# Turning second and left blocks ahead of the next maxima, in a fused attention and MLP kernel

## The chip, the cores and the metric

The kernel runs on one core of one Trainium2 chip. The metric is the device time of one execution in microseconds (us). TensorE (PE) multiplies matrices, VectorE (DVE), ScalarE (ACT) and GpSimd (POOL) work element by element, and SyncE (SP) issues most of the DMA transfers. Each engine works through a queue of its own, and semaphores hold an instruction until its inputs are there.

## The reference

Two stages follow each other. The first is attention with a threshold, for 8 batches, 8 heads, 576 rows and a head size of 64, all in float32; the second is an MLP with a squared ReLU on the 4608 tokens that come out.

```
scores = scale * q @ k.T                                   # 576 x 576 for each head
thresh = max(scores, axis=-1) - tau
scores = where(scores >= thresh, scores, -1e9)
attn   = exp(scores - max(scores)); attn = attn / (sum(attn) + 1e-9)
x      = attn @ v                                          # -> 4608 x 512 tokens
out    = relu(x @ w_in) ** 2 @ w_out                       # w_in 512 x 2048, w_out 2048 x 512
```

## The kernel before, in words

The attention is done in **visits**. A visit takes two heads of a batch (`HP` = 4 such pairs of heads for each batch). The 576 rows are cut into four blocks of 128 (`NBLK` = 4) and a rest of 64. A **step** `s` handles one block of one visit: `steps[s]` is `(visit, block)`, and block number 4 stands for the rest. From visit 12 on (`paired`), two visits are taken together, and the rests of both visits make one block of 128 rows, the **left block**, which is the first step of the pair. A pair of visits so has nine steps: the left block, then blocks 0 to 3 of one visit and 0 to 3 of the other. These are the late steps, written by `late_step`; they begin at about 243 us of the profile. There are 12 such pairs, so 108 late steps, and some more after them that finish what is open. `NST` is the number of steps, and `END` is the step in which the last values are multiplied.

For each block and each of the two heads the work goes through the engines in this order:

- **Scores** (`scores_of_two`, L296, PE): the matmuls of q with k, into PSUM. An even block brings the scores of itself and of the odd block behind it; the odd step has none of its own.
- **Maxima** (`maxima`, L317, DVE): two reductions over 576 scores.
- **Exponents** (`exponents`, L340 to L343, ACT): two small operations on the maxima, and the exponential of both heads, with the maxima as bias.
- **Threshold** (`threshold`, L355 to L360, DVE): compares the scores with the threshold, multiplies the exponents with that, and sums.
- **Division** (`divide`, L365 and L367, POOL).
- **Turn** (`turn_blocks`, L459 to L469, DVE): transposes the divided block in squares of 32 x 32 into `turned`. A full block takes three or four transposes, a left block three.
- **Set-aside** (`set_aside`, L436): when the second block of two is turned, POOL issues a DMA that writes both from `turned` to DRAM, 1152 KB. `turn_last(s)` calls the turn for the block of step `s - 1` and, after an odd block, the set-aside.
- **Placing** (`place_blocks`): DMAs from SP read the two blocks back, in the order that the matmul needs, into `wT` (L477); a left block goes there straight from `turned` (L486).
- **Values** (`mix`, L530, PE): weights times v. ACT copies the result to `xT`, the tokens of the MLP (L513 to L524).

Between these, PE works on the MLP in **pieces** of some 1.8 us (`piece`, `fill`): sums of products with `w_in` (`unit`, L693) and with `w_out` (`product`, L799). What follows a piece on other engines is issued one piece later (`after`): ACT copies and squares (L701 to L729), additions on DVE (L705, L816 to L837), and sums of factors on POOL and DVE (L624), of which some stand in two waiting lists and are taken out one at a time (`some_later("gpsimd")`, `some_later("vector")`).

The order of each engine's instructions is the order in which the Python code issues them; no scheduler changes it. In a late step before the change, the code asks for the scores, the work behind the last piece, the maxima, one waiting operation of POOL, the exponents, then the turn of the last step's block if that was an odd block or a left block (`first`), pieces, threshold and division. If the last step's block was even, its turn comes later, behind this step's threshold. Only two buffers hold the weights of the blocks in turn (`w_slots`), so the exponents of step `s` need the turn of step `s - 2`.

Of the kernel before, what the change touches and what calls it, by code (L numbers as in the profile page):

```python
# [19 lines left out]
def kernel(  # L20
# [17 lines left out]
    NBLK = S // P  # L38
# [245 lines left out]
    def area(u, odd):  # L284
        at = AT[u, odd][0]
        return big[:, at:at + S].rearrange("p (h k) -> p h k", h=2)

    def scores_of_two(s):


        vis, i = steps[s]

        def term(u, odd, second_part, lhsT, keys, to=slice(0, P)):
            at, cut = AT[u, odd]
            x0, x1 = (cut, S) if second_part else (0, cut)
            nc.tensor.matmul(big[to, at + x0:at + x1], lhsT, keys[u * D:(u + 1) * D, x0:x1], start=True, stop=True)  # L296

        if i == NBLK:
            for x in range(2):
                for v_ in range(2):  # L300
                    for u in range(2):
                        cols = slice(v_ * D, (v_ + 1) * D)
                        term(u, 0, x != u, qmid[u * D:(u + 1) * D, cols], kT[v_], cols)
            return
        for at_, (u, odd, x) in enumerate(((1, 1, 0), (0, 0, 0), (1, 0, 1), (0, 0, 1), (1, 0, 0), (0, 1, 0), (1, 1, 1), (0, 1, 1))):
            at = (i + odd) * P
            term(u, odd, x, qT[u * D:(u + 1) * D, at:at + P], kT[vis % 2])
            if at_ == 0:
                nc.scalar.copy(seen, big[:, AT[1, 1][0]:AT[1, 1][0] + 1])

    def maxima(s, sc):
        vis, i = steps[s]
        n = len(sc)
        st = stats[s % len(stats)]
        mx = st[:, 0, 0:n]
        for u in range(n):
            nc.vector.tensor_reduce(out=mx[:, u:u + 1], in_=sc[u], axis=AX.XY, op=ALU.max)  # L317
        w = w_slots[(s - first_dma) % (2 if by_dma(vis) else 3)][:, 0:n, :]
        weights[vis, i] = w, sc, st
# [17 lines left out]
    def exponents(vis, i):  # L337
        w, sc, st = weights[vis, i]
        mx, thr, bias = (st[:, j, 0:len(sc)] for j in range(3))
        nc.scalar.activation(out=bias, in_=mx, func=AF.Copy, scale=-SCALE)  # L340
        nc.scalar.activation(out=thr, in_=mx, func=AF.Identity, bias=ntau8)
        for u in range(len(sc)):
            nc.scalar.activation(out=w[:, u, :].rearrange("p (h k) -> p h k", h=2), in_=sc[u],  # L343
                                 func=AF.Exp, bias=bias[:, u:u + 1], scale=SCALE)
# [88 lines left out]
    def set_aside(vis, pair):  # L433

        t = aside[len(outside) % 4]
        nc.gpsimd.dma_start(out=t, in_=turned[:, 0:NB])  # L436
        outside[vis, pair] = t.rearrange("(b r) (j x) -> r j b x", r=32, j=4)

    def turn_blocks(vis, i):

        w = weights[vis, i][0]
        two = i < NBLK
        M = KB - 2
        if not two or i % 2 == 0:
            lo = NB if paired(vis) else NB + NB // 2
            blocks[vis, i // 2] = (turned[:, 0:NB].rearrange("p (j c u q) -> p c j u q", j=4, u=2, q=32) if two  # L450
                                   else turned[:, lo:lo + NB // 2].rearrange("p (k q) -> p k q", q=32))
        wb = blocks[vis, i // 2]
        move = nc.vector.transpose
        if two:
            wb = wb[:, :, :, i % 2, :]
            whole_, rest_ = (w[:, :, x0 * 32:x1 * 32].rearrange("p u (c j q) -> p u c j q", q=32, j=n)
                             for x0, x1, n in ((0, M, 4), (M, KB, 2)))
            h = M // 4
            move(wb[:, 0:h, :, :], whole_[:, 0, :, :, :])  # L459
            if i < 2:  # L460
                move(wb[:, h, :, :].rearrange("p (u j) q -> p u j q", u=2), rest_[:, :, 0, :, :])
            else:
                move(wb[:, h, 2:4, :], rest_[:, 0, 0, :, :])
                move(wb[:, h, 0:2, :], rest_[:, 1, 0, :, :])
            move(wb[:, h + 1:, :, :], whole_[:, 1, :, :, :])  # L465
            return
        parts = [(0, 0, KB, 0), (1, M, KB, KB), (1, 0, M, KB + 2)] if paired(vis) else [(0, 0, KB, 2), (0, M, KB, 0)]
        for u, k0, k1, at in parts:
            move(wb[:, at:at + k1 - k0, :], w[:, u, k0 * 32:k1 * 32].rearrange("p (k q) -> p k q", q=32))  # L469
# [183 lines left out]
    def some_later(engine):  # L653
        if later[engine]:
            make(*later[engine].popleft())
# [201 lines left out]
    steps = [(n, i) for n in range(len(visits)) for i in visits[n][1]]  # L857
    NST = len(steps)

    def by_dma(n):  # L860

        return n >= 3 * HP - 1
# [7 lines left out]
    for s, (n, i) in enumerate(steps):  # L870
# [5 lines left out]
        if i in mixed:  # L876
            first, lag = mixed[i]
# [38 lines left out]
    def add_chunk(j):  # L916
        waiting.extend(pieces_of(j))
        whole.add(j)
# [27 lines left out]
    def after():  # L946
        now = state["last"]
        state["last"] = []
        for fn in state["then"]:
            state["last"] += fn() or []  # L950
        state["then"] = []
        for fn in now:
            fn()

    def piece():
        _, fn, *what = waiting.popleft()
        state["left"] -= PIECE_US
        state["made"] += 1
        if fn is mlp_out or what[0] <= PLAIN and what[1] == 0:
            after()  # L960
        then = fn(*what)
        after()
        state["then"] = then
        if state["step"] >= NST:
            some_later("vector")
            some_later("gpsimd")

    def fill(us):
        state["left"] += us
        while waiting and state["left"] >= PIECE_US / 2 and waiting[0][0] <= state["usable"]:  # L970
            piece()
        state["left"] = min(state["left"], PIECE_US)
# [77 lines left out]
    def turn_last(s):  # L1050
        if s <= NST:
            turn_blocks(*steps[s - 1])
            n, i = steps[s - 1]
            if i % 2 and by_dma(n) and goes_out(n, i // 2):
                set_aside(n, i // 2)

    def goes_out(n, pair):

        return pair < NBLK // 2
# [5 lines left out]
    def late_step(s):  # L1065

        on = s < NST
        odd = on and steps[s][1] % 2 == 1
        if on:
            n, i = steps[s]  # L1070
            if not odd:
                scores_of_two(s)
            after()
            maxima(s, [area(u, odd) for u in range(2)])
            some_later("gpsimd")
            exponents(n, i)
        first = s > NST or steps[s - 1][1] % 2 == 1 or steps[s - 1][1] == NBLK
        if first:
            turn_last(s)
        valued = s in mixes and s < END  # L1080

        todo = list(place_at[s])

        def place(all_):
            for what in list(todo):
                if all_ or not goes_out(*what[:2]):
                    place_blocks(*what)
                    todo.remove(what)

        if not valued:  # L1090
            place(False)

        def values():
            if s in mixes:
                while (visits[mixes[s][0]][0] // HP + 1) * S - RING > read_to["x"]:
                    piece()
                mix(*mixes[s])
                for j in chunk_at.get(s, ()):
                    add_chunk(j)

        if s == END:
            values()
        quarter = rate(s) / 4 if s < END else 1e9
        made = state["made"]
        fill(quarter)
        some_later("gpsimd")
        after()
        if on:
            threshold(n, i)
            divide(n, i)  # L1110
        if first:
            some_later("vector")
        fill(quarter)
        after()
        if not first:
            some_later("vector")
            turn_last(s)
        for fn in prep_at[s] + load_at[s]:
            fn()
        some_later("gpsimd")  # L1120
        if valued:
            at_least(1, made)
            made = state["made"]
            values()
        some_loads()
        place(True)
        some_later("vector")
        some_loads()
        fill(quarter)
        some_loads()  # L1130
        fill(quarter)
        some_loads()
        if valued:
            at_least(2, made)
            state["left"] = max(state["left"], -PIECE_US / 2)
# [55 lines left out]
    for s in range(END + 1):  # L1191
# [12 lines left out]
        on = s < NST  # L1204
# [130 lines left out]
```

## Time and profile before

| What | Value |
|---|---|
| Median of 3 runs | 1320.76 us (1320.71 to 1320.98) |
| The profiled execution | 1320.85 us, of which the span is 1319.1 us |
| TensorE | busy 1290.9 us, 98% of the span |
| VectorE | busy 936.9 us, 71% |
| GpSimd | busy 776.2 us, 59% |
| ScalarE | busy 585.4 us, 44% |
| POOL's wait at the set-aside for the turn (L436 for L465) | 177.5 us in 41 waits |
| DVE's wait at the maxima for the scores (L317 for L296) | 60.6 us in 47 waits |
| DVE's wait at the threshold for the exponents (L355 for L343) | 85.6 us in 58 waits |
| SP's wait at the placing for the set-aside (L477 for its landing) | 294.7 us in 42 waits |

A row of the timeline gives the start in us from the beginning of the span, the length, the engine, the line of the kernel, the operation with what it writes and reads, and in brackets how long the engine was idle before and what ended that. Matmuls overlap in the array, and their ends are modelled. Idle time of an engine costs nothing in itself; only what delays the last instruction does.

### The profile page before, as it was taken

How to read it: one execution, taken by the hardware profiler on the slowest of the kernel's cores; microseconds unless marked ns; L12 is line 12 of the kernel's file. 1: busy time of each engine (PE TensorE's matmuls, PEld its weight loads, DVE VectorE, ACT ScalarE, POOL GpSimd, SP SyncE). 2: the span in 40 equal slices, each digit the busy share in tenths (PEclk: the TensorE clock that was granted, in tenths of full speed). 3: DMA queues.
4: the chain of work that ended last, by engine and by line, in shares of the span. 5: the costliest groups of instructions: out<-in, count | busy, mean ns of one | idle time of the engine just before them, and what ended most of it. 6: DMA issues, size and time to landing. Idle time of an engine off the chain costs nothing.

```text
span 1319.1 us, 24730 instructions
## 1 busy us (share of the span) xinstructions
PE 1290.9 (98%) x8862; PEld 1070.6 (81%) x8862; DVE 936.9 (71%) x2034; ACT 585.4 (44%) x1353; POOL 776.2 (59%) x908
## 2 busy tenths in 40 slices
PE   7999999999999999999999999999999999999997
PEld 6676557897888888797978888888887988889997
DVE  6899776777777788788776877878686877522131
ACT  4887763244343526253435343525353434331331
POOL 3788874775747475556574746656574737455351
PEclk9999999999999999999999999999999999999999
DMA  6765431777777878686666768667676866520000
GB/s 127 156 181 145 126 73 60 145 173 168 165 173 178 181 177 186 143 200 160 170 157 158 158 154 187 172 137 185 146 173 139 198 162 161 144 53 9 9 17 17
DMA packets 320907, 185.48 MB, mean 141 GB/s; under 512 B 282224, under 2 KB 282256, under 8 KB 314384
## 3 DMA queue, kind: packets, MB, share of 16 engines
q1 hardware_dynamic: 309120, 115.78, 46.4%
q0 software_dynamic: 10000, 67.92, 12.9%
q8 instruction: 70, 1.15, 0.4%
q14 instruction: 53, 0.43, 0.1%
q10 hardware_dynamic: 1664, 0.21, 0.1%
HBM read 108.04 MB, written 68.42 MB: 134 GB/s over the span
## 4 chain that ended last, share of the span: by engine, by line
PE 83%; DVE 6%; DMA 3%; ACT 2%; issue 1%; POOL 1%; SPq 0%; DVEq 0%; POOLq 0%; ACTq 0%
PE big L693 29%; PE big L799 28%; PE big L530 10%; PE big L296 8%; PE big L579 3%; PE big L764 2%; PE big L280 2%; DVE st L317 1%; DMA wT<-aside 1%; DMA aside<-turned 1%; PE big L414 1%; DVE w L355 1%; ACT w L343 1%; DVE turned L154 0%; PE big L273 0%
## 5 line engine op out<-in xcount | busy, mean ns | idle before, releaser
L355 DVE SCALAR_TENSOR_TENSOR w<-big,st,w 128x576 f32<-128x576 f32 x269 | 207.4, 805 | 87.6 <-ACT w L343 85.6
L317 DVE TENSOR_REDUCE st<-big 128x1 f32<-128x576 f32 x288 | 204.1, 747 | 85.3 <-PE big L296 60.6
L367 POOL TENSOR_SCALAR w<-w,st 128x576 f32<-128x576 f32 x269 | 244.2, 916 | 29.4 <-DVE st L360 24.6
L799 PE MATMUL big<-wo,gsum 128*128 128x256 f32 x1088 | 243.8, 382 | 0.0
L799 PEld LDWEIGHTS big<-wo,gsum 128*128 128x128 f32 x1088 | 204.4, 190 | 37.0 <-issue 7.6
L693 PE MATMUL big<-xT,w_in_sb 128*128 128x128 f32 x1536 | 187.4, 277 | 1.5 <-DVE g L705 1.4
L693 PEld LDWEIGHTS big<-xT,w_in_sb 128*128 128x128 f32 x1536 | 178.5, 192 | 10.8 <-issue 7.7
L799 PE MATMUL big<-wo,g 128*128 128x256 f32 x816 | 185.3, 382 | 0.1
L343 ACT ACTIVATE w<-big,st 128x576 f32<-128x576 f32 x255 | 174.4, 735 | 0.2 <-issue 0.2
L799 PEld LDWEIGHTS big<-wo,g 128*128 128x128 f32 x816 | 151.6, 190 | 26.2 <-issue 6.5
L530 PE MATMUL big<-wT,vs 128*64 128x256 f32 (+5 forms) x1420 | 159.5, 389 | 4.9 <-DMA wT<-aside 3.5
L530 PEld LDWEIGHTS big<-wT,vs 128*64 128x64 f32 (+1 forms) x1420 | 86.0, 136 | 70.1 <-issue 20.8
L340 ACT ACTIVATE st<-st 128x2 f32<-128x2 f32 (+1 forms) x137 | 28.1, 205 | 253.3 <-DVE st L317 252.1
L365 POOL TENSOR_SCALAR st<-st 128x2 f32<-128x2 f32 (+1 forms) x148 | 35.6, 241 | 177.7 <-DVE w L355 167.1
L436 POOL DMA_DIRECT2D aside<-turned x50 | 29.9, 597 | 177.5 <-DVE turned L465 177.5
L705 DVE TENSOR_TENSOR g<-big,g 128x512 f32<-128x512 f32 x96 | 64.6, 676 | 83.7 <-PE big L693 78.1
L296 PE MATMUL big<-kT,qT 64*128 64x256 f32 (+3 forms) x768 | 107.0, 416 | 0.0
L296 PEld LDWEIGHTS big<-kT,qT 64*128 64x128 f32 x768 | 84.6, 186 | 14.5 <-issue 5.0
L701 ACT ACTIVATE g<-g 128x512 f32<-128x512 f32 x96 | 60.4, 630 | 63.5 <-DVE g L705 63.4
L569 POOL TENSOR_TENSOR gsum<-g 128x512 f32<-128x512 f32 x34 | 46.1, 1356 | 69.9 <-ACT g L702 69.6
L702 ACT ACTIVATE g<-g 128x512 f32<-128x512 f32 x128 | 80.9, 632 | 4.0
L459 DVE STREAM_TRANSPOSE turned<-w 128x512 f32<-128x512 f32 x100 | 70.2, 702 | 0.3 <-issue 0.3
(119 smaller groups left out, 2058.1 us busy)
## 6 DMA issues: line engine op xcount, KB each, us to landing
aside<-turned POOLq DMA_DIRECT2D x50, 1152.0 KB, 4.8
wT<-aside SPq DMA_DIRECT2D x200, 288.0 KB, 5.4
vs<-in_v_dram SPq DMA_DIRECT2D x72, 128.0 KB, 5.7
wo<-in_moe_w_in_dram SPq DMA_DIRECT2D x16, 512.0 KB, 4.8
wo<-in_moe_w_out_dram SPq DMA_DIRECT2D x16, 512.0 KB, 3.5
out_dram<-osb POOLq DMA_DIRECT2D x32, 256.0 KB, 3.9
kl<-in_k_dram SPq DMA_DIRECT2D x113, 72.0 KB, 2.8
ql<-in_q_dram SPq DMA_DIRECT2D x112, 72.0 KB, 5.7
```

The costliest lines, as they stand in the source:

```text
L296: nc.tensor.matmul(big[to, at + x0:at + x1], lhsT, keys[u * D:(u + 1) * D, x0:x1], start=True, stop=True)
L317: nc.vector.tensor_reduce(out=mx[:, u:u + 1], in_=sc[u], axis=AX.XY, op=ALU.max)
L343: nc.scalar.activation(out=w[:, u, :].rearrange("p (h k) -> p h k", h=2), in_=sc[u], func=AF.Exp, bias=bias[:, u:u + 1], scale=SCALE)
L355: nc.vector.scalar_tensor_tensor(out=wu, in0=sc[u], scalar=thr[:, u:u + 1], in1=wu, op0=ALU.is_ge, op1=ALU.mult, accum_out=sm[:, u:u + 1])
L367: nc.gpsimd.tensor_scalar(out=w[:, u, :], in0=w[:, u, :], scalar1=z[:, u:u + 1], scalar2=rcp[:, u:u + 1], op0=ALU.add, op1=ALU.mult)
L459: move(wb[:, 0:h, :, :], whole_[:, 0, :, :, :])
L530: nc.tensor.matmul(ps[u * D:(u + 1) * D, :], vs[n % 2][rows, u * (NBLK + 1) + c, :], wT[rows, at // REST:(at + ps.shape[1]) // REST, NBLK ...
L693: nc.tensor.matmul(to[:, f, :], factor(j, p, q, c)[:, f * P:(f + 1) * P], part[:, c, :], start=(p in "125" and f == 0 and c == 0), stop=(p ...
L701: nc.scalar.activation(out=to, in_=to if src is None else src, func=AF.Relu)
L702: nc.scalar.activation(out=to, in_=to, func=AF.Square)
L705: nc.vector.tensor_tensor(out=x, in0=to, in1=x, op=ALU.add)
L799: nc.tensor.matmul(to, left[:, f, :], wo[:, slot, f, :], start=(f == 0), stop=(f == HF - 1))
```

## The change

In `late_step`, the turn of a second block (an odd one) or of a left block is issued ahead of the maxima of the next step, and so also ahead of one waiting operation of POOL and of the exponents. The turn of an even block stays where it is. The very last block, whose turn was in the step behind the last one, is turned at the end of the last step, directly behind the turn of the block before it. PE, ACT and SP get the same instructions in the same order as before.

```diff
             if not odd:
                 scores_of_two(s)
             after()
+        first = s > NST or steps[s - 1][1] % 2 == 1 or steps[s - 1][1] == NBLK
+        if first and s != NST:
+            turn_last(s)
+        if on:
             maxima(s, [area(u, odd) for u in range(2)])
             some_later("gpsimd")
             exponents(n, i)
-        first = s > NST or steps[s - 1][1] % 2 == 1 or steps[s - 1][1] == NBLK
-        if first:
-            turn_last(s)
         valued = s in mixes and s < END
...
         if not first:
             some_later("vector")
             turn_last(s)
+            if s == NST - 1:
+                turn_last(NST)
         for fn in prep_at[s] + load_at[s]:
             fn()
```

## The prediction

> **What bounds the kernel now.** I read the page first, for the engine that is full; then the table of windows, for the stage in which it is full; then PE's own waits in that stage; then the timeline around some of the moved turns.
>
> ```profile
> PE 1290.9 (98%) x8862; PEld 1070.6 (81%) x8862; DVE 936.9 (71%) x2034; ACT 585.4 (44%) x1353; POOL 776.2 (59%) x908
> ```
>
> TensorE is full. In the window from 243 to 1158 us, the stage of paired visits that the change touches, it is busy for 910.71 of 915.00 us, so 4.29 us are idle there. From 1164.6 on only the MLP's matmuls are left, and PE runs them through. A stop of PE ahead of that point is therefore added to the time at the full, and a stop that is taken away is gained at the full. The question is which PE waits end sooner and which new ones arise.
>
> ```profile
> PE big L530 <- DMA wT<-aside: 2.8, 2, 1.6
> PE big L693 <- DVE g L705: 1.0, 1, 1.0
> PE big L693 <- POOL g L624: 0.7, 1, 0.7
> ```
>
> These are PE's waits from 500 us on (total us, times, longest). The first is what turning sooner could shorten; the timeline shows its two members at 549.96 (1.22 us) and 1162.07 (1.58 us), and one more of 0.69 us at 407.23.
>
> [...] at 825.27 ScalarE has stood idle 4.39 us for a maximum. So a late maximum holds up every copy behind it. [...] the page's DMA issues show a median of 4.8. The earlier start thus moves the landing, and does not shorten it.
>
> **The change part by part.** No instruction is added or removed. On PE, ACT and SP the order is the same; on DVE and POOL only places change.
>
> *Part 1, 60 turns go ahead of maxima.* They are one left block from the visit before the stage, 12 left blocks of the pairs, and 47 second blocks (48 less the very last). One turn lasts 1.49 us (L459 0.70, L461 0.27, L465 0.67, overlapping a little), 1.54 with four pieces.
>
> ```profile
> 823.53 0.38 DVE L837 TENSOR_TENSOR osb<-big,osb 128x256 f32<-128x256 f32 x1
> 823.84 1.40 DVE L317 TENSOR_REDUCE st<-big 128x1 f32<-128x576 f32 x2
> 825.17 0.68 DVE L459 STREAM_TRANSPOSE turned<-w 128x512 f32<-128x512 f32 x1
> 825.78 0.26 DVE L461 STREAM_TRANSPOSE turned<-w 128x128 f32<-128x128 f32 x1
> 825.98 0.66 DVE L465 STREAM_TRANSPOSE turned<-w 128x512 f32<-128x512 f32 x1
> 826.57 0.77 DVE L355 SCALAR_TENSOR_TENSOR w<-big,st,w 128x576 f32<-128x576 f32 x1
> ```
>
> ```profile
> 825.27 0.21 ACT L340 ACTIVATE st<-st 128x2 f32<-128x2 f32 x1 [4.39 <-DVE st L317]
> 825.57 1.37 ACT L343 ACTIVATE w<-big,st 128x576 f32<-128x576 f32 x2
> 826.82 0.59 ACT L713 COPY g<-big 128x512 f32<-128x512 f32 x1
> ```
>
> In this place (columns: start, length, engine, line) VectorE turns while ScalarE makes the exponents: the turn is hidden under 1.9 us of ScalarE work, and the threshold follows it at once. With the turn first, maxima, exponents and the copy L713 all come 1.5 us later, VectorE then waits for the exponents, and the threshold comes 1.3 us later. PE needs L713's copy at 827.56, 0.15 us after its end.
>
> What hides the moved turn in its new place is VectorE's wait for the scores. For each of the 60 I took from the timeline when VectorE was free, when the division (L367) was done, and when the maximum began; the new maximum begins a turn after the later of the first two. In 9 places the wait covers the turn; in 51 the maximum comes later; the mean over all is 0.93 us. The threshold, which today starts when the turn ends and about 0.3 us after the first exponent, comes 0.58 us later in the mean. VectorE is busy 698 of 915 us here, so most of this is caught up in its waits for PE. It costs where PE needs something queued behind: a copy of ScalarE behind the exponents (L713, L718, L725), a VectorE result behind the threshold (L705, L837, kT), or GpSimd work behind the division (L624).
>
> I set each such lateness against the time between the result's end and PE's start on it, in the trace of before. PE has 659 waits on these engines in the stage and after; on DVE 18, ACT 18 and POOL 7 results lie less than 1 us ahead of their use. Where the lateness is more than that, the rest is a stop of PE, at (us): 278.5 L837 0.49; 436.5 L718 0.87; 507.4 L718 0.93; 761.1 kT 1.10; 767.6 L725 1.05; 827.6 L713 1.44; 893.2 L624 1.05; 905.5 L713 0.60; 965.8 L713 1.55; 1042.2 L718 0.59; three small ones 0.27. Sum: 9.9 us lost.
>
> *The DMAs of part 1.* Each of the 47 second blocks has a 1152 KB set-aside (L436) that GpSimd issues; it also goes ahead of one queued GpSimd operation (some 1.3 us for an L624). The turn ends 2.0 us sooner in the mean, so GpSimd waits less at L436 (177.5 us in all today), but what stood between may now wait for the turn. SP's queue keeps its order, and most of its waits are for these landings (294.7 us in 42 waits at L477), so it comes free sooner. For the two transfers that PE waits for, the turn starts 2.13 us earlier (392.79 and 535.00 today), more than 0.69 and 1.22: both stops go. Gain 1.9 us.
>
> *Part 2, the last block.* Today its turn stands behind L816, which waits for PE:
>
> ```profile
> 1144.41 0.42 DVE L816 TENSOR_TENSOR osb<-big,held 128x256 f32<-128x256 f32 x1 [2.96 <-PE big L799]
> 1144.75 0.70 DVE L459 STREAM_TRANSPOSE turned<-w 128x512 f32<-128x512 f32 x1
> ```
>
> ```profile
> 1146.59 0.60 POOL L436 DMA_DIRECT2D aside<-turned  x1 [4.82 <-DVE turned L465]
> ```
>
> The division ends at 1141.77 and the turn before it at 1141.45, so it can start at 1141.8, 2.9 us sooner. GpSimd is idle, and SP has already waited at L477. PE's stop of 1.58 us at 1162.07 goes unless the transfer is slowed: this one took 7.7 us to land beside four L477 transfers and will overlap them longer. Bounds of the gain: 0 and 1.58; I take 1.58, as 1.3 us are to spare. Work behind the turn on VectorE is L816, which waits for PE until 1144.4 anyway: cost nothing.
>
> *Sum.* 9.9 - 1.9 - 1.6 = +6.4 us on the profiled execution's 1320.85 (span 1319.1, and 1.75 around), which is 0.09 above the median of 1320.76. That gives 1327.2; I say 1327.
>
> The lateness that I took for the turn is bounded below by nothing (VectorE's slack takes it, as in 9 places) and above by the full 1.54 us. The waits of the turn on GpSimd are not fully shown: in 18 of 60 places the division ends after VectorE is free, by 1.2 us at 900.86, and it may itself be late after a late threshold. Bounds of the lost sum: 2 us, if a stop of PE gives the next places room and VectorE catches up, and 15, if lateness also reaches the second maximum of a pair and the next scores (L296 starts within 1.6 us of the end of the threshold it waits for in 19 places).
>
> **Rivals.** *Hidden, and the transfers gain* (ends on the other side): VectorE waits for scores ahead of maxima in 49 of the 60 places, 60.6 us at L317 over the whole run, and the turn fits in; PE loses under 0.8 us and wins 3.5: 1317.3. Against it are the 11 places without any such wait, where there is no room, and the short reserves at 827.6 and 965.8. It decides if the losses stay under 0.8 us. Chance 0.09.
>
> *Halved*: the stops lie close together (761 and 768, 893 and 905, 1022 to 1042) and the first makes room for the second; about 4 to 5 us lost, 3.5 won: 1322. For it: the stop at 761.1 moves all that PE needs later by 1.1 us. Chance 0.16.
>
> *Runs on*: the division comes late too, GpSimd holds the turn, and VectorE stops with everything behind it: 15 lost, 3.5 won, 1332. For it: GpSimd works without a wait from 880 to 888. Chance 0.15.
>
> That the change does not do what it says is excluded: in the built program's order the turns stand ahead of the maxima.
>
> **How the numbers follow.** My forecast has 0.60. A measurement of this kernel can tell 0.2%, or 2.6 us, from no change, so faster is under 1318.1 and slower over 1323.4. Slower: forecast 0.60, the late rival 0.15, and a little of the halved one, 0.77 in all; same 0.14; faster 0.09. The range runs from 1319.5 (losses of 2 us beside the gains, the lower bound) to 1332.5 (losses of 15 with gains of 3.5).
>
> **What would show it.** Right: PE waits of 0.5 to 1.5 us at L693 behind ACT copies L713, L718 and L725; VectorE's wait at L355 for ACT rising from 85.6 us by some 35 (60 times about 0.6); L436's wait on the turn falling below 177.5; the wait for wT<-aside gone from PE. Wrong: PE idle in the stage still at 4 us, or the L530 stops still there.

## The result, and the profile after

| | Median | Runs |
|---|---|---|
| Before | 1320.74 us | 4 runs, 1319.98 to 1320.98 |
| After | 1329.99 us | 4 runs, 1329.04 to 1331.56 |

The change makes the kernel slower by 0.7%: the ratio of after to before is 1.0072, with a 95% interval of 1.0055 to 1.009. The profiled execution of after took 1330.07 us, of which the span is 1328.3 us, against 1320.85 and 1319.1 before. The forecast was 1327 us, slower.

The first line of the page of after gives each engine's busy time, its share of the span and its instructions:

```profile
PE 1296.2 (98%) x8862; PEld 1073.7 (81%) x8862; DVE 941.6 (71%) x2034; ACT 581.7 (44%) x1353; POOL 776.9 (58%) x908
```

TensorE has 5.3 us more of busy time for the same 8862 matmuls. Two windows of 3.41 us at half clock, at 59 and 428 us, make some 2.9 us of it (the delays of 1.27 and 1.62 us in the table below). I put the rest down to parts of stops: the modelled end of the matmul ahead of a stop covers a little of it (at 827.6 PE becomes 1.28 us late, but counts as idle for 0.99). In the stage itself, from 243 to 1166 us of after, PE is busy for 912.91 of 923.00 us, so 10.09 us are idle, where it was 4.29. Of PE's waits in after, over the whole run, those that the change bears on (us in total, times, longest):

```profile
PE big L693 <- DVE g L705: 2.4, 1, 2.4
...
PE big L693 <- ACT g L713: 2.1, 2, 1.1
PE big L693 <- POOL g L624: 2.0, 3, 0.9
...
PE big L693 <- ACT g L718: 1.3, 2, 0.8
```

The wait for `wT<-aside`, 3.5 us in three waits before, is gone altogether. In its place stand waits for copies of ScalarE and for GpSimd's sums, as forecast (one of 1.1 us for kT is in the same list), and one stop of 2.4 us behind VectorE's L705, which was not in the forecast. The waits of all engines in after show how the order of work shifted:

```profile
DVE w L355 <- ACT w L343: 140.3, 114, 3.8
...
POOL aside L436 <- DVE turned L465: 88.1, 32, 6.3
...
DVE st L317 <- PE big L296: 11.9, 11, 1.9
```

VectorE's wait for the scores (L317) fell from 60.6 to 11.9 us: the turns now stand in that wait. Its wait for the exponents (L355) rose from 85.6 to 140.3 us: the turns no longer stand in that one. The same work has moved from one hole to another, and what lies between the two holes (maxima, exponents, the copies behind them) is late. GpSimd waits 89 us less at the set-aside, and 88 us more at L365 for the threshold (255.3 us for 167.1).

The place that the prediction showed, in the timeline of after (start, length, engine, line; in brackets the wait and what ended it):

```profile
830.42 0.69 DVE L459 STREAM_TRANSPOSE turned<-w 128x512 f32<-128x512 f32 x1
...
831.82 1.38 DVE L317 TENSOR_REDUCE st<-big 128x1 f32<-128x576 f32 x2
...
833.53 1.36 ACT L343 ACTIVATE w<-big,st 128x576 f32<-128x576 f32 x2
...
834.29 0.82 DVE L355 SCALAR_TENSOR_TENSOR w<-big,st,w 128x576 f32<-128x576 f32 x1 [1.09 <-ACT w L343]
...
834.78 0.59 ACT L713 COPY g<-big 128x512 f32<-128x512 f32 x1
...
835.42 2.05 PE L693 MATMUL big<-t,g 128*128 128x128 f32 x16 [0.99 <-ACT g L713]
```

The turn stands ahead of the maxima. L343 begins 1.71 us behind their start, as before (1.73), but VectorE has nothing to do until then and waits 1.09 us. The copy L713 ends at 835.37, just ahead of PE's start: PE has stopped for 0.99 us. Part 2 of the change in the same view:

```profile
1152.39 0.67 DVE L459 STREAM_TRANSPOSE turned<-w 128x512 f32<-128x512 f32 x1
...
1154.21 0.60 POOL L436 DMA_DIRECT2D aside<-turned  x1 [1.41 <-DVE turned L465]
...
1155.44 0.42 DVE L816 TENSOR_TENSOR osb<-big,held 128x256 f32<-128x256 f32 x1 [1.53 <-PE big L799]
```

The last turn follows the one before it (its L465 ends at 1152.47) without a gap, and stands ahead of L816; the set-aside goes out 1.2 us ahead of L816, where it was 2.2 us behind it.

**Where the 9.25 us come from.** PE's instructions have the same order in both kernels, so the start of each can be set against the start of the same one before. The shift between the two grows or falls only in a few places. At the end it is 9.25 us. That the medians differ by the same figure (1329.99 - 1320.74) is chance, since the four runs of after spread over 2.5 us. Places are named by their time before, with the line whose wait changed there.

| Place (us) | Forecast | Measured |
|---|---|---|
| 278.5, L837 | +0.49 | +0.34 |
| 373.9, scores L296 | none | +0.68 |
| 407.2, transfer | -0.69 | -0.81 |
| 423.4, L705 | none | +1.94, and +1.62 behind it |
| 436.5, L718 | +0.87 | 0 |
| 507.4, L718 | +0.93 | +0.79 |
| 550.0, transfer | -1.22 | -1.43 |
| 761.1, kT | +1.10 | +1.28 |
| 767.6, L725 | +1.05 | +0.93 |
| 827.6, L713 | +1.44 | +1.28 |
| 893.2, L624 | +1.05 | +1.15 |
| 905.5, L713 | +0.60 | 0 |
| 965.8 L713, and 968.8 behind it | +1.55 | +1.37 - 0.94 |
| 1032.9, L624 | not named | +0.56 |
| three small ones, places not given | +0.27 | not told apart |
| 1042.2, L718 | +0.59 | +1.04 |
| 1162.0, transfer | -1.58 | -1.78 |
| 445.4 to 493.6, and 820.0 | none | -0.26 + 0.22 |
| 59.5 to 60.6, ahead of the change | none | +1.27 |
| Sum | +6.4 | +9.25 |

The last place lies in the first stage, which the change does not touch. It is a variation between runs: it is there in three of the fourteen traces of this study, two of them of experiments. So about 8 us of this pair of traces are the change's own; the interval of the ratio, 7.3 to 11.9 us, holds this.

The largest term is the one that the forecast lacked, at 423 us. The timelines show what happened there. Before:

```profile
419.23 1.28 POOL L624 TENSOR_TENSOR gsum<-w_in_sb,g 128x512 f32<-128x512 f32 x1
...
419.91 1.16 DVE L624 TENSOR_TENSOR gsum<-w_in_sb 128x512 f32<-128x512 f32 x1
...
423.43 2.05 PE L693 MATMUL big<-xT,w_in_sb 128*128 128x128 f32 x16 [0.44 <-DVE g L705]
```

After:

```profile
421.43 2.50 POOL L624 TENSOR_TENSOR gsum<-w_in_sb,g 128x512 f32<-128x512 f32 x2
...
421.90 2.58 DVE L624 TENSOR_TENSOR gsum<-w_in_sb 128x512 f32<-128x512 f32 x1
...
426.85 2.90 PE L693 MATMUL big<-xT,w_in_sb 128*128 128x128 f32 x16 [2.38 <-DVE g L705]
```

GpSimd makes two sums L624 in both; before, the first began at 417.43. VectorE's own L624 took 1.16 us before and takes 2.58 after; it ends 0.56 us after the end of GpSimd's second one in both (421.07 and 420.51; 424.48 and 423.93). Then come one more L624, L705, and PE, which has stood 2.38 us instead of 0.44. The 16 matmuls from 426.85 on take 2.90 us instead of 2.05. The table of windows tells why, with three stretches of after (start, end and length; busy us and instructions of PE, PEld, DVE, ACT and POOL; then the granted clock):

```profile
424.44:427.85 3.41, 1.04 (x10) 1.01 (x10) 3.41 (x6) 0.99 (x2) 3.24 (x5) 1.00 0.77 235
427.85:431.26 3.41, 3.41 (x19) 3.41 (x18) 1.68 (x4) 2.90 (x7) 2.18 (x2) 0.50 1.01 234
431.26:434.68 3.41, 3.41 (x30) 3.27 (x31) 3.07 (x10) 0.00 (x0) 1.85 (x3) 1.00 1.17 197
```

In the window that holds the stop, PE is busy for 1.04 of 3.41 us. In the next, just as long, it runs at a clock of 0.50 and has 19 matmuls, where the window after it has 30. That is the 1.62 us behind the stop, and it is the busy time that grew.

### The profile page after: what moved, and what is told of

Its sections match the earlier page's. It is cut to its first block, busy times and chain, and to the rows that moved or that the text cites. A ratio compares the mean times of both kernels' runs of the same rounds, so it can differ in the third digit from the quotient of the medians.

```text
span 1328.3 us, 24730 instructions
## 1 busy us (share of the span) xinstructions
PE 1296.2 (98%) x8862; PEld 1073.7 (81%) x8862; DVE 941.6 (71%) x2034; ACT 581.7 (44%) x1353; POOL 776.9 (58%) x908
## 3 DMA queue, kind: packets, MB, share of 16 engines
q8 instruction: 70, 1.15, 0.4%
## 4 chain that ended last, share of the span: by engine, by line
PE 79%; DVE 10%; ACT 3%; issue 2%; POOL 1%; DVEq 0%; ACTq 0%; POOLq 0%
PE big L799 27%; PE big L693 26%; PE big L530 10%; PE big L296 7%; PE big L579 3%; DVE st L317 3%; PE big L280 2%; DVE w L355 2%; PE big L764 2%; ACT w L343 2%; PE big L414 1%; DVE gsum L823 1%; DVE turned L465 1%; DVE turned L459 1%; POOL w L367 0%
## 5 line engine op out<-in xcount | busy, mean ns | idle before, releaser
L355 DVE SCALAR_TENSOR_TENSOR w<-big,st,w 128x576 f32<-128x576 f32 x269 | 209.6, 815 | 142.1 <-ACT w L343 140.3
L367 POOL TENSOR_SCALAR w<-w,st 128x576 f32<-128x576 f32 x269 | 244.6, 918 | 30.9 <-DVE st L360 27.0
L317 DVE TENSOR_REDUCE st<-big 128x1 f32<-128x576 f32 x288 | 202.6, 741 | 37.1 <-PE big L280 23.0
L693 PE MATMUL big<-xT,w_in_sb 128*128 128x128 f32 x1536 | 188.6, 278 | 3.8 <-DVE g L705 2.4
L365 POOL TENSOR_SCALAR st<-st 128x2 f32<-128x2 f32 (+1 forms) x148 | 35.6, 241 | 264.8 <-DVE w L355 255.3
L693 PEld LDWEIGHTS big<-xT,w_in_sb 128*128 128x128 f32 x1536 | 179.2, 192 | 13.3 <-issue 7.3
L343 ACT ACTIVATE w<-big,st 128x576 f32<-128x576 f32 x255 | 173.9, 732 | 0.2 <-issue 0.2
L705 DVE TENSOR_TENSOR g<-big,g 128x512 f32<-128x512 f32 x96 | 65.1, 680 | 80.4 <-PE big L693 74.1
L296 PE MATMUL big<-kT,qT 64*128 64x256 f32 (+3 forms) x768 | 107.5, 416 | 0.2 <-DVE w L355 0.2
L296 PEld LDWEIGHTS big<-kT,qT 64*128 64x128 f32 x768 | 84.7, 186 | 15.2 <-issue 3.6
L436 POOL DMA_DIRECT2D aside<-turned x50 | 29.8, 595 | 94.5 <-DVE turned L465 88.1
```

What stands on the lines that cost most here:

```text
L355: nc.vector.scalar_tensor_tensor(out=wu, in0=sc[u], scalar=thr[:, u:u + 1], in1=wu, op0=ALU.is_ge, op1=ALU.mult, accum_out=sm[:, u:u + 1])
L367: nc.gpsimd.tensor_scalar(out=w[:, u, :], in0=w[:, u, :], scalar1=z[:, u:u + 1], scalar2=rcp[:, u:u + 1], op0=ALU.add, op1=ALU.mult)
L693: nc.tensor.matmul(to[:, f, :], factor(j, p, q, c)[:, f * P:(f + 1) * P], part[:, c, :], start=(p in "125" and f == 0 and c == 0), stop=(p ...
L705: nc.vector.tensor_tensor(out=x, in0=to, in1=x, op=ALU.add)
```

## The experiments

The expectations call a turn a transpose, and a sum L624 a multiply-add. Two questions were open: whether the listed stops are really caused by the ten moves that the forecast put them down to, and what brought the stop at 423 us. In the experiments the moves of part 1 are counted from 0 to 59; `firsts` is the list of their steps. All ratios are to runs of the kernel before on the same chip, with 95% intervals.

### The ten moves, back and alone

The ten moves behind the ten listed stops were left in their old place, and all else of the change kept:

```diff
+    firsts = [s for s in range(first_late, NST) if steps[s - 1][1] % 2 == 1 or steps[s - 1][1] == NBLK]
...
-        if first and s != NST:
+        ahead = first and s < NST and firsts.index(s) not in (2, 13, 18, 34, 35, 39, 43, 44, 48, 53)
+        if ahead:
             turn_last(s)
...
             exponents(n, i)
+        if first and s != NST and not ahead:
+            turn_last(s)
```

> The change, but at the ten moves where the prediction placed a stop of TensorE (numbers 2, 13, 18, 34, 35, 39, 43, 44, 48 and 53 of the 60) the turn stands behind the maxima again; 50 moves and the last block's turn remain. Theory (lateness costs only where TensorE needs something queued behind, so the loss sits in these ten places): in the trace after, the stops there sum to about 8.2 us, and a stop of 0.9 at 968.8 comes back, so 7 us less than the change, about 1323. Rival (the lateness is spread over all moves, each costing its share of some 13 us): a sixth of that, 2 us less, about 1328.

Then those ten alone went ahead (`in` for `not in`), without part 2:

> Only these ten turns are ahead of the maxima; the other 50 and the last block stay as before. Theory of the ten places: about 7 us slower than before, 1328, without the two gains at the values (407 and 550) and at the end. Rival of spread lateness: 2 us slower, 1323.

Measured: with the ten taken back, 1319.98 us (12 runs), ratio 0.9999 (0.9991 to 1.0008). The ten alone: 1328.92 us (4 runs), ratio 1.0061 (1.0046 to 1.0076). Of PE's waits with the ten alone:

```profile
PE big L530 <- DMA wT<-aside: 3.0, 3, 1.2
```

Ten moves of sixty make a loss nearly as large as the whole, with the same waits for L713 as in after (2.1 us in two), and leave the transfers' stops. Shift by place: 436.5 +0.73, 507.4 +0.79, 761.1 +1.18, 767.6 +0.94, 827.6 +1.27, 893.2 +1.17, 965.8 +1.41 less 0.95 behind it, 1042.2 +0.43. Together that is 7.0 us at eight of the ten places. At 278.5 only 0.18 came, at 905.5 nothing, and 0.44 at 445.4, which no list had.

The other fifty and part 2 cancel out, but not because each costs nothing. In their trace the transfers' stops are gone (-0.90, -1.42 and -1.79 us at 407, 550 and 1162), while the stop at 423 is there at its full, 2.51 us (+2.04, and +1.4 of half clock behind it), and the scores at 373.9 and the sum at 1032.9 are late by 0.59 and 0.57. The kernel is 3 us faster than I had expected, and only one of these shows in the traces: the profiled run of 1322.01 us is 8.06 below after's 1330.07, where 7 were expected, and some 0.8 of that lie in the first stage. The median is 2.0 us lower still. Each run has its own granted clock on record: the three at 0.995 or 0.996, the profiled one among them, took 1322.0 to 1322.6 us, the nine at 0.997 or 0.998 took 1318.7 to 1320.4. So most runs seem to be without one of the half-clock windows; no trace of such a run is kept, so this is not shown.

### Part 1 alone, part 2 alone

```diff
         if not first:
             some_later("vector")
             turn_last(s)
-            if s == NST - 1:
-                turn_last(NST)
```

with the last turn at its old place in the step behind is part 1 alone; the turn of before with these two lines is part 2 alone.

> The 60 moves without the last block's earlier turn. Theory: TensorE's stop of about 1.6 us for the last wT transfer is back, so 1.6 to 2 us slower than the change: about 1331.8. Rival (the earlier turn only overlaps the transfer with others, and the last values wait all the same): as the change, 1330.

> The last block's turn directly behind the one before it, and no other move. Theory: the stop of 1.58 us at 1162 is gone and nothing else differs: 1319.0, 0.12% faster than before. Rival: the set-aside, overlapping the transfers before it, lands no sooner: 1320.7.

Part 1 alone took 1331.6 us (4 runs, 1327.04 to 1331.88), ratio 1.0071 (1.0047 to 1.0094); the stop at the last transfer is back, 1.38 us. Part 2 alone took 1319.05 us (20 runs), ratio 0.999 (0.9984 to 0.9997); in its trace only this stop is gone. So part 2 is worth 1.3 to 1.6 us, as forecast, and the loss is part 1's. In the profiled run of part 1 alone the stop at 423 is there with 2.44 us, but no half clock follows it; one follows two stops for GpSimd's L624 at 900 us instead (PE loses 2.8 us there, where the others with the ten moves lose some 1.2), as it does in the kernel of the next section with the set-aside at its old place.

### The stop at 423 us: two theories that fell

My first theory was that GpSimd's set-aside, moved ahead of one queued sum, had left its two sums L624 back to back, and VectorE's sum without a place between them. In the first test the turns go ahead as in the change, but the set-aside keeps its old place:

```diff
-        if first and s != NST:
-            turn_last(s)
+        if first and s < NST:
+            turn_blocks(*steps[s - 1])
...
             some_later("gpsimd")
             exponents(n, i)
+            if first and steps[s - 1][1] % 2:
+                set_aside(steps[s - 1][0], steps[s - 1][1] // 2)
```

> VectorE's transposes go ahead of the next maxima as in the change, but the set-aside on GpSimd keeps its old place in GpSimd's order, one multiply-add later. Theory (the stop of 2.4 us at 423 us comes of GpSimd running two multiply-adds back to back beside VectorE's, which takes 2.58 us in place of 1.16): that stop goes, with it 2.0 us and the half-clock window behind it of about 1.6 us, and the kernel takes about 1326.4 us. Rival (the stop comes of VectorE's own order, the transpose ahead of the maxima): it stays, and the kernel takes 1330 us like the change.

My second theory put the stop down to the move beside it, no. 12, at 415 us. It was taken back along with the ten, and tried alone:

```diff
+        ahead = first and s < NST and firsts.index(s) not in (2, 12, 13, 18, 34, 35, 39, 43, 44, 48, 53)
```

> As the kernel with ten moves taken back, with move no. 12 (at 415 us) taken back too. Theory (the stop at 423 us hangs on that one move): 1319.98 - 2.0 = 1318 us, and to 1316.5 us where the half-clock window behind that stop goes with it. Rival (it hangs on the moves ahead of it, which put VectorE and GpSimd at another time): it stays, 1320 us.

```diff
+        ahead = first and s < NST and firsts.index(s) == 12
```

> The kernel before with move no. 12 (at 415 us) alone. Theory (that one move brings the stop at 423 us): 1320.5 + 2.0 = 1322.5 us, and up to 1324 us with a half-clock window behind the stop. Rival (the prediction's tally, which gave that move no cost): 1320.5 us.

Measured: with the set-aside at its old place 1329.15 us (4 runs), ratio 1.006 (1.0046 to 1.0074); with no. 12 taken back too 1320.51 us (13 runs), ratio 1.0002 (0.9993 to 1.001); with no. 12 alone 1320.49 us (12 runs), ratio 1.0002 (0.9994 to 1.0011). Both theories fell. The timeline with the set-aside at its old place:

```profile
419.49 2.63 DVE L624 TENSOR_TENSOR gsum<-w_in_sb 128x512 f32<-128x512 f32 x1
...
420.28 1.29 POOL L624 TENSOR_TENSOR gsum<-w_in_sb,g 128x512 f32<-128x512 f32 x1
...
424.48 2.05 PE L693 MATMUL big<-xT,w_in_sb 128*128 128x128 f32 x16 [2.49 <-DVE g L705]
```

And with move no. 12 alone:

```profile
417.64 2.51 POOL L624 TENSOR_TENSOR gsum<-w_in_sb,g 128x512 f32<-128x512 f32 x2
...
419.41 1.30 DVE L624 TENSOR_TENSOR gsum<-w_in_sb 128x512 f32<-128x512 f32 x1
...
423.07 2.05 PE L693 MATMUL big<-xT,w_in_sb 128*128 128x128 f32 x16 [0.39 <-DVE g L705]
```

In the first, GpSimd has its old order, with the set-aside between the sums (at 419.70), and the stop stays at 2.49 us. In the second the sums are back to back, and the stop is 0.39 us. What differs is the time: GpSimd's second sum ends 7.0 us after PE's matmuls L693 of that unit begin in the first (421.57 less 414.57), 4.9 us after in the second (420.15 less 415.27). So GpSimd is late in the first, and the lateness comes from further up.

### The stop at 423 us: what brings it

GpSimd's chain to that sum has no room in the trace before: from the scaling L367 at 403.30 on it never waits more than 0.26 us until its second sum ends at 420.51. So what is late at 403 is late at 421. Its longest wait there, in the trace before:

```profile
403.30 2.68 POOL L367 TENSOR_SCALAR w<-w,st 128x576 f32<-128x576 f32 x2 [0.26 <-DVE st L360]
```

The move in front of it is no. 11, whose turn at 401 us has three pieces of L469. It is the turn of a left block, not of a second block, as an expectation below calls it. Before:

```profile
398.46 1.42 DVE L317 TENSOR_REDUCE st<-big 128x1 f32<-128x576 f32 x2 [1.09 <-PE big L296]
...
399.80 1.49 DVE L469 STREAM_TRANSPOSE turned<-w 128x576 f32<-128x576 f32 x3
```

After:

```profile
400.60 1.64 DVE L469 STREAM_TRANSPOSE turned<-w 128x576 f32<-128x576 f32 x3 [0.64 <-POOL w L367]
...
402.16 1.39 DVE L317 TENSOR_REDUCE st<-big 128x1 f32<-128x576 f32 x2
...
404.64 0.82 DVE L355 SCALAR_TENSOR_TENSOR w<-big,st,w 128x576 f32<-128x576 f32 x1 [1.09 <-ACT w L343]
```

The turn waits 0.64 us for GpSimd's scaling, then goes ahead, then come the maxima, the exponents, and the threshold at 404.64: 3.43 us later than before (401.21), while PE is 2.3 us later there. So the division behind it on GpSimd is 1.1 us late against PE. The other suspect is PE itself: through move no. 10 it no longer stops at 407 us, and so comes 0.81 us sooner to a result that is no sooner. The stop before plus both is 0.44 + 1.1 + 0.81 = 2.35, against 2.38 measured. To test that, no. 11 was taken back from the change, no. 11 was taken back beside the ten, and each of the two was moved alone:

```diff
+        ahead = first and s < NST and firsts.index(s) != 11
```

> The change, with one move of 60 taken back: no. 11, the second block at 401 us, whose transposes wait 0.65 us for GpSimd's scaling and then run ahead of the maxima. Theory (this wait and these transposes put the softmax of the next block late, with it GpSimd's queue by some 1.4 us, so that VectorE's multiply-add at 422 us falls on two of GpSimd's): the stop of 2.4 us at 423 us falls to about 1.05 us, as in the kernel with two moves, the half-clock window behind it goes, and the time is 1330 - 1.3 - 1.6 = 1327 us. Rival (the stop is the work of all the moves before it together): it stays over 2 us and the time at 1330 us.

> As the kernel with ten moves taken back (1320 us), with no. 11 taken back too; part 2 is in. Theory: 1320 - 1.3 - 1.4 = 1317.3 us, about the time of the kernel with two moves. Rival: the stop at 423 us stays, 1320 us.

```diff
+        ahead = first and s < NST and firsts.index(s) == 11
```

> The kernel before with move no. 11 alone. Theory: GpSimd's chain is 1.4 us late at 417 us, VectorE's multiply-add at 420 us takes about 2.5 us in place of 1.16, and TensorE stops 1.8 us in place of 0.44 at 423 us: 1320.5 + 1.4 = 1321.9 us, and 1323.5 us if a half-clock window follows. Rival (the stop needs the earlier arrival of TensorE that move no. 10 brings): 0.4 us more at most, 1320.9 us.

> The kernel before with move no. 10 alone, which takes the stop of 0.69 us at 407 us away. Theory (what is gained there is handed back at 423 us, where TensorE comes earlier to a result of VectorE that is no earlier): -0.6 us at 407 us, +0.6 us at 423 us, 1320.5 us in all. Rival (the gain is kept): 1319.8 us and no longer stop at 423 us.

Move no. 11 alone:

```profile
419.67 2.22 DVE L624 TENSOR_TENSOR gsum<-w_in_sb 128x512 f32<-128x512 f32 x1
...
424.26 2.05 PE L693 MATMUL big<-xT,w_in_sb 128*128 128x128 f32 x16 [1.51 <-DVE g L705]
```

Move no. 10 alone:

```profile
419.25 2.04 DVE L624 TENSOR_TENSOR gsum<-w_in_sb 128x512 f32<-128x512 f32 x1
...
423.66 2.05 PE L693 MATMUL big<-xT,w_in_sb 128*128 128x128 f32 x16 [1.32 <-DVE g L705]
```

| Kernel | Stop at 423 us | Median | Ratio |
|---|---|---|---|
| No. 11 alone | 1.51 us | 1319.77 us (12 runs) | 1.0002 (0.9993 to 1.001) |
| No. 10 alone | 1.32 us | 1319.39 us (12 runs) | 0.9996 (0.9988 to 1.0005) |
| Change without no. 11 | 1.22 us | 1328.42 us (4 runs) | 1.0067 (1.0053 to 1.0082) |
| Ten and no. 11 back | 1.32 us | 1319.06 us (13 runs) | 0.9994 (0.9985 to 1.0002) |

Each of the two alone lengthens the stop of 0.44 us by about 1 us, and both make it 2.4 to 2.5. No. 11 alone costs 1.07 us at that place, where I had expected 1.4. No. 10 alone wins 0.88 us at 407 (the shift goes from +0.22 to -0.66) and hands back 0.89 at 423 (to +0.23): nothing is left of the gain. These are readings of the traces; the intervals of the two single moves reach from 0.9988 to 1.001, so their medians can't tell 1 us from nothing. In the two kernels without no. 11 no half clock follows the stop. Yet their medians fall by only 1.6 us (1329.99 to 1328.42) and 0.9 us (1319.98 to 1319.06), where I had expected 2.9 and 2.7; the intervals of both pairs overlap, so neither step is clear of noise. The traces suggest why less came than expected. In the change without no. 11, the shift at 423 is 0.79 instead of 3.56, 2.8 us less; but at 436.5 and 445.4, where after has none, it now grows by 0.73 and 0.45. PE, no longer late, meets those two late results. That leaves 1.6 us at these places. In the kernel with the ten back those two stops can't come, but its median lies 2 us under its profiled run and so seems to be without the half clock already; then only the shorter stop is saved, 2.04 - 0.89 = 1.15 us.

### Two moves and part 2

Only the two moves whose transfers PE waited for, no. 10 and no. 20 (at 391 and 534 us), and part 2:

```diff
+        ahead = first and s < NST and firsts.index(s) in (10, 20)
```

> Part 2 of the change and only two moves of 60, the left-block steps no. 10 and 20 (at 391 and 534 us), whose transposed weights TensorE waited for at 407 and 550 us. Theory (those two stops are gained by these two moves alone): 0.8 and 1.4 us less beside part 2's gain, 1320.5 - 1.6 - 2.2 = 1316.7 us. Rival (the transfer comes sooner only because earlier steps are moved too): the stops stay, 1319 us.

Measured: 1317.39 us (11 runs), ratio 0.9979 (0.997 to 0.9988), the fastest kernel of the study. The two moves gain by themselves, without the earlier ones. But the gain over part 2 alone is 1.7 us by the medians, 1.5 by the ratios, and not 2.2:

```profile
PE big L693 <- DVE g L705: 2.0, 2, 1.1
```

No wait for a transfer is left, and the longest wait for L705 is 1.1 us: the 0.60 us won at 407 came back as 0.62 at 423. What stays is the 1.4 us at 550 and the 1.8 at 1162.

## Why the prediction was right, and where not

**Right: the direction, and the mechanism.** TensorE is full, the moved turn stands in the place of maxima and exponents, and PE stops behind copies of ScalarE. VectorE's wait at L355 rose by 55 us where some 35 were forecast, L436's fell below 177.5, and the wait for `wT<-aside` went. The time of 1329.99 lies in the range, 3 us above the forecast. (The ends of the range come to 1319.3 and 1332.3 from its own losses and gains, 0.2 below those stated.)

**Right: the transfers.** All three stops went, for 4.0 us of shift where 3.5 were forecast. Part 2 alone shows its part of it. That an earlier start moves a set-aside's landing and does not shorten it was my estimate; a set-aside of 1152 KB took 4.8 us to land in the median of before, and 5.1 in that of after. The risk that the last set-aside would be slowed by its neighbours was real, but small: it took 8.51 us to land instead of 7.70, and was issued 3.4 us sooner, against L816.

**Too large: the ten listed stops.** They were given 9.67 us, and the shift at their places is 7.24 (the 0.94 won back at 968.8 counted against 965.8). Two came to nothing. At 436.5 the stop at 423 and the half clock behind it had already put PE late; in the traces without half clock there (the ten alone, part 1 alone, the set-aside at its old place, the change without no. 11) the place has its 0.72 to 0.74 us. At 905.5 none of the kernels shows it, and in all that have the ten moves PE loses some 1.2 us at 893 first (2.8 where half clock follows). At 968.8 PE used to wait 0.95 us for L705 and, being late, no longer does. That is the rival called halved, in part: one stop makes room for the next.

**Left out: the stop at 423 us, 3.56 us.** The step that failed is the tally of stops. Each of its ten listed stops lies between its move and the next moved turn; no. 11's lateness lives on in GpSimd's queue for 20 us, past the turn of no. 12, and the list has nothing for it. (Of the rivals, runs on comes nearest to this: there a late division makes GpSimd late.) And the tally took PE's arrival as before, so it booked the 0.7 us at 407 as won, though the result that PE needs at 423 does not come sooner. Both were measured, at about 1 us each; the half-clock window, 1.62 us, was on no list at all. Its net price is less: without it, the stops at 436.5 and 445.4 come (1.18 us). The trace of before showed what was needed: GpSimd without a wait over 0.26 us from 403 to 420, and a stop of 0.44 us at 423 that had no reserve.

**Left out or too small: three others.** The scores at 373.9 (+0.68), the sum at 1032.9 (+0.56, which the forecast doesn't name, unless it is one of its three small ones of 0.27 together), and L718 at 1042.2 (+1.04 for 0.59). Their causes stay open; 373.9 and 1032.9 are there whenever the fifty moves are, and not with the ten alone.

**The balance.** Of the 2.8 us between 6.4 and 9.25, the ten stops gave -2.4, the other stops +2.9 (3.14 without the half clock, less 0.27), the half-clock window +1.6, the gains -0.5, and the run's own variation in the first stage +1.3. The forecast came as near as it did partly by luck: its errors point both ways. With the ten stops sized as measured, it would have come to 4.0 us.

## What to carry to other kernels

A turn, or any work, that is moved from one wait of an engine into another is free only if what lies between the two waits has reserve; count the engines queued behind it, not the busy shares. A stop taken away from a full engine is a gain only up to the next result that this engine needs and that comes no sooner: follow the arrival as far as that result. And move only the few instructions whose earlier end is waited for: two moves of sixty and the last turn gained 0.2%, all sixty and the last turn lost 0.7%.

## What the runs showed of the hardware

**Half clock behind stops of TensorE.** The traces have the clock from about 8 us on. While PE still had work, it was 0.50 in three stretches of 3.41 us in after, from 18.25, 59.21 and 427.85 us, and in one in before, from 18.06 us. Those of after start 40.96 and 368.64 us apart, which is 12 and 108 times 3.413 us. In the 3.41 us ahead of them PE was idle for 2.46, 1.76 and 2.37 us in after, and for 2.45 us in before (with modelled ends of matmuls). Where the two traces are cut into stretches of 3.41 us that fit these starts, one more stretch within the clock's record has over 1.42 us of idle time: at 55.6 us of before it is 1.76 us, as in after, but full clock followed. The two stretches at half clock that before does not have cost 1.27 and 1.62 us of PE's time: at 428 us eight pairs of matmuls took 0.43 us each instead of 0.22. So the stop of 2.38 us was followed by a loss of 1.62 us more. The length of a stop alone did not decide it: in part 1 alone no half clock followed the stop of 2.44 us, and with the set-aside at its old place the 16 matmuls behind the stop of 2.49 us took 2.05 us, as before. What does decide is not shown.

**VectorE behind GpSimd.** VectorE's L624 at 420 us ended 0.55 to 0.56 us after the end of GpSimd's second L624 in before, in after and in ten of the experiments, whether it lasted 1.16 us (before), 2.58 (after) or 3.16 (eleven moves back); where no GpSimd work lay beside it in the trace before (four rows, the first at 914.8 us), an L624 of VectorE took 0.65 to 0.69 us. A place at 622 us of before is like it: VectorE's row of 1.31 us ends 0.55 us behind the first of two sums L624 of GpSimd, and the second sum, right behind it, takes 1.72 us instead of 1.28. In the kernel with eleven moves back, VectorE's row begins during GpSimd's first sum, which ends 0.5 us ahead of the second, and it still ends behind the second. With no. 11 alone and with no. 10 alone its row begins 0.38 and 0.20 us ahead of the second sum, beside the set-aside, and still ends behind it. Why VectorE's sum takes longer beside GpSimd's, and why it did not end in between there, is not shown.
